# A ring of four output buffers and a newly searched issue order in a fused attention and feed-forward kernel

## The chip, the cores and the metric

The kernel runs on one core of a Trainium2 chip. Its time is device time in microseconds (us). Before the change it takes 350.42 us, the median of three runs (350.24 to 351.2). A core has a matrix engine, TensorE (PE in the profile, with its weight loads listed apart as PEld); a vector engine, VectorE (DVE); a scalar engine for activations, ScalarE (ACT); GpSimd (POOL) and SyncE (SP), which here do little but issue transfers. Each engine works through its own queue in order. PE writes into PSUM, a memory of eight banks of 128 x 512 float32; all other buffers are in SBUF, 128 partitions wide.

## The reference

Two stages. First an attention whose softmax is replaced by features: with `q`, `k`, `v` of 8 batches x 8 heads x 576 positions x 64 and `w_phi` of 64 x 128,

```python
def phi(x):
    proj = np.einsum('bhsd,df->bhsf', x, w_phi)
    proj = proj - np.max(np.abs(proj), axis=-1, keepdims=True)
    return np.concatenate([np.exp(proj), np.exp(-proj)], axis=-1)
q_p, k_p = (phi(q), phi(k))
kv = np.einsum('bhsf,bhsd->bhfd', k_p, v)
z = np.sum(k_p, axis=2)
num = np.einsum('bhsf,bhfd->bhsd', q_p, kv)
den = np.einsum('bhsf,bhf->bhs', q_p, z)[..., None] + 1e-06
attn = num / den
```

Then the heads are put side by side, giving 4608 tokens of 512, and a feed-forward layer follows: `h = max(x @ w_in, 0)`, `out = (h * h) @ w_out`, with `w_in` of 512 x 2048 and `w_out` of 2048 x 512. The output is 4608 x 512 in float32.

## The kernel before

The function builds a plan of 1738 operations and then issues them in a fixed order. Each `add` names an engine, a cost, the buffers read (`r`) and written (`w`), and the PSUM bank that the operation opens or closes. `plan.arrange` applies four tables that an offline search has left at the end of the file. `ORDER` is the order of issue of all operations, so it sets the queue of each engine. `BASES` gives the PSUM bank of each opened group. `STATES` chooses between ACT and DVE for 231 copies and relus that either can do (`either`). `GATES` names, for each load on POOL, the operation that it has to wait for. A fifth table, `FILL`, puts runs of dummy matmuls on zeros ahead of named operations: `85: (0, 26)` is 26 of them into bank 0 ahead of operation 85. Operations are named by their number in the plan in what follows.

An operation's buffers come from the framework, which adds the waits: an instruction that uses a PSUM bank or an SBUF buffer waits for what used it before in the order of issue, where one of the two writes, and two engines' accesses to one PSUM bank are put one behind the other even where both only read.

**Attention**, one batch of 576 positions x 8 heads at a time (18 blocks of 128 columns). `xk`, `xq`, `xv` are the loads (L245 and others, POOL). `kT` and `qT` hold the transposed inputs: for batches 0 and 1 PE transposes them (L316) and DVE or ACT copies them out; for batches 2 to 7 one DMA transpose each, issued on SP, does it. L342 is the projection of four blocks into two PSUM banks; its two row halves use 64 of the array's rows at a time. Of each projection DVE takes the maximum of the absolute value (L397 for keys into `mk`, L501 and L534 for queries into `mq`) and ACT the two exponentials (L403 into `kp` and `kn`; L547 into `qf`, or from a second projection with the operands exchanged, L572, the exponentials of L587 into `qpn`). The value rows are scaled by exp of the maxima (L416 and L422 on ACT, L430 on DVE, into `va`), L463 makes `kv`, which is copied out by L192 or L190. L651 multiplies query features with `kv`, the positive half first; DVE scales that half in PSUM (L663), the negative half is added, DVE takes the reciprocal of the denominators (L673) and writes the tokens `xo` (L677). A DMA transpose on SP (L711, operations `Xx`) brings `xo` into `xT`, for batch 0 PE and a copy do (the first tile of all in two halves, `out_halves`).

**Feed-forward**: chunk c is the first 512 tokens of batch c; the ninth chunk is the 8 x 64 positions left over, gathered in `xS`. Per chunk 16 groups of four matmuls (L797) make the hidden layer, ACT or DVE applies the relu into `hr` (L774, L776), DVE squares it into `h2` (L783). For chunk 0 the groups are cut smaller, so that they can begin with the first tokens (L822 in halves, L808, L836). Four groups of 16 matmuls (L891) make an output tile of 128 tokens; L192 or L190 copies it out of PSUM into a buffer of the ring `ot` of three, and SP stores it (L909, L906 for the ninth chunk). The very last tile of 36 is made in two unequal halves (L855), copied by ACT (L871) and DVE (L869) into a buffer of its own, `otl`, and stored in four pieces over SP and ACT (L878).

The chunks and the next batch's attention are woven into one another by `ORDER`. In SP's queue the stores of output tiles stand between the transposes; around 66 to 80 us the order there is query transpose 396, transposes of tokens 297 and 306, store 519, transpose of tokens 315, store 537.

## Time and the profile before

The profiled execution took 351.15 us; its span, from the first to the last instruction, is 349.2 us.

| | |
|---|---|
| median of three runs | 350.42 us (350.24 to 351.2) |
| profiled execution | 351.15 us, span 349.2 us |
| PE, matmuls | 336.7 us, 96% of the span |
| DVE | 272.0 us, 78% |
| ACT | 229.6 us, 66% |
| POOL | 96.2 us, 28% |
| moved to and from memory | 46.2 MB (36.77 MB read, 9.44 MB written), 132 GB/s over the span |

Busy shares are those of an engine's instructions over the whole span, and a busy PE also counts dummy matmuls and the modelled ends of pipelined ones. Idle time ahead of an instruction is put down to what ended it. In a view of groups each line has the busy time, the mean duration in nanoseconds, and the idle time ahead with its most frequent releaser. In the timeline a square bracket holds the idle time ahead of an instruction and what ended it; a `q` behind an engine's name is its queue of transfers. In the table by stages the columns are PE, weight loads, DVE, ACT and POOL (busy us and instructions in brackets), then granted PE clock, share of the DMA engines and GB/s.

### The profile page before, as it was taken

To read this page: it belongs to the slowest core of one execution; us is meant where nothing else is said; L and a number is where in the kernel's file an instruction comes from. 1 tells how busy PE (TensorE), PEld (TensorE's weight loads), DVE (VectorE), ACT (ScalarE), POOL (GpSimd) and SP (SyncE) were. 2 spreads that over 40 slices of the span, in tenths; PEclk is the share of its full clock that TensorE was granted. 3 is DMA by queue.
4 is the path that set the end of the run, shared out by engine and by line. 5 is a ranking of instruction groups with operands and counts; after the bars stand their busy time and mean duration, and the time that the engine had idled before them with its cause. 6 is when DMAs were issued, how large, how long until landed. Compare 5 with 4: busy or idle time off the path is not lost.

```text
span 349.2 us, 8405 instructions
## 1 busy us (share of the span) xinstructions
PE 336.7 (96%) x3323; PEld 192.3 (55%) x3353; DVE 272.0 (78%) x518; ACT 229.6 (66%) x434; POOL 96.2 (28%) x144
## 2 busy tenths in 40 slices
PE   6999999999999999999999999999999999999994
PEld 5878866544654555446555554465555554444443
DVE  2999999889988979898989995998889735653251
ACT  3999897789978995877698788584785403232011
POOL 8844352283361835060600130360000000000000
PEclk9999999999999999999999999999999999999998
DMA  8999999898997999899999999999785422000025
GB/s 90 178 201 200 203 120 147 137 194 129 146 163 159 148 155 147 173 163 210 165 196 189 227 154 150 206 142 161 157 153 145 90 47 98 32 0 30 0 92 121
DMA packets 133623, 49.05 MB, mean 140 GB/s; under 512 B 102096, under 2 KB 129104, under 8 KB 133584
## 3 DMA queue, kind: packets, MB, share of 16 engines
q0 software_dynamic: 45232, 18.36, 45.9%
q1 hardware_dynamic: 88112, 29.99, 42.6%
q8 instruction: 26, 0.43, 0.5%
q10 hardware_dynamic: 240, 0.16, 0.1%
q14 instruction: 13, 0.11, 0.1%
HBM read 36.77 MB, written 9.44 MB: 132 GB/s over the span
## 4 chain that ended last, share of the span: by engine, by line
PE 84%; DVE 7%; DMA 3%; ACT 3%; issue 2%; POOL 1%; POOLq 0%; DVEq 0%; ACTq 0%
PE psum L891 32%; PE psum L797 31%; PE psum L651 5%; PE psum L342 5%; PE psum L458 4%; DVE va L430 2%; PE psum L836 2%; DMA xk<-in_k_dram 1%; DMA xT<-xo 1%; PE psum L572 1%; PE psum L822 1%; PE psum L808 1%; DVE mq L501 1%; PE psum L855 1%; PE psum L463 1%
## 5 line engine op out<-in xcount | busy, mean ns | idle before, releaser
L891 PE MATMUL psum<-wout,h 128*128 128x512 bf16 x530 | 129.6, 379 | 2.3 <-issue 1.1
L797 PE MATMUL psum<-xT,win 128*128 128x512 bf16 x448 | 106.7, 379 | 0.3 <-DMA xT<-xo 0.2
L774 ACT ACTIVATE hr<-psum 128x512 bf16<-128x512 f32 x97 | 56.5, 598 | 53.9 <-PE psum L797 28.4
L891 PEld LDWEIGHTS <-h 128*128 128x128 bf16 x560 | 50.7, 97 | 54.9 <-issue 0.6
L797 PEld LDWEIGHTS <-win 128*128 128x128 bf16 x512 | 47.2, 97 | 52.5 <-issue 1.8
L783 DVE TENSOR_TENSOR h<-hr 128x512 bf16<-128x512 bf16 x144 | 56.7, 415 | 12.4 <-ACT hr L774 11.8
L776 DVE TENSOR_SCALAR hr<-psum 128x512 bf16<-128x512 f32 x47 | 32.0, 686 | 19.2 <-PE psum L797 17.7
L547 ACT ACTIVATE qf<-psum 128x1024 bf16<-128x1024 f32 (+1 forms) x40 | 36.2, 937 | 10.2 <-DVE mq L534 9.4
L403 ACT ACTIVATE kp<-psum 128x1024 bf16<-128x1024 f32 (+1 forms) x35 | 32.9, 941 | 12.8 <-DVE mk L397 12.5
L397 DVE TENSOR_REDUCE mk<-psum 128x8 f32<-128x1024 f32 (+1 forms) x35 | 38.7, 1110 | 2.5 <-PE psum L342 2.3
L587 ACT ACTIVATE qpn<-psum 128x1024 bf16<-128x1024 f32 (+1 forms) x40 | 36.5, 945 | 3.4 <-PE psum L572 3.4
L651 PEld LDWEIGHTS <-qpn 128*128 128x128 bf16 x624 | 27.6, 97 | 13.3 <-issue 0.8
L430 DVE TENSOR_TENSOR va<-xv,va 64x256 bf16<-64x256 bf16 (+2 forms) x66 | 30.1, 470 | 4.1 <-ACT va L422 3.5
L403 ACT ACTIVATE kn<-psum 128x1024 bf16<-128x1024 f32 (+1 forms) x35 | 32.7, 938 | 0.0
L663 DVE TENSOR_TENSOR psum<-psum,en 128x520 f32<-128x520 f32 (+1 forms) x39 | 27.3, 701 | 6.9 <-PE psum L651 5.2
L245 POOL DMA_DIRECT2D xv<-in_v_dram x27 | 19.8, 742 | 39.2 <-ACT va L416 11.6
L651 PE MATMUL psum<-kv,qpn 128*128 128x65 bf16 x624 | 30.2, 193 | 0.2
L245 POOL DMA_DIRECT2D xk<-in_k_dram x28 | 20.4, 742 | 35.4 <-PE psum L463 16.4
L677 DVE TENSOR_TENSOR xo<-psum,rden 128x512 bf16<-128x512 f32 (+1 forms) x39 | 26.7, 686 | 1.0 <-DVE rden L673 0.2
L534 DVE TENSOR_REDUCE mq<-psum 128x8 f32<-128x1024 f32 (+1 forms) x20 | 22.2, 1113 | 2.0 <-PE psum L342 1.1
L192 ACT ACTIVATE ot<-psum 128x512 f32<-128x512 f32 x20 | 12.0, 598 | 17.8 <-PE psum L891 15.8
L501 DVE TENSOR_REDUCE mq<-psum 128x8 f32<-128x1024 f32 (+1 forms) x20 | 22.0, 1110 | 1.8 <-PE psum L342 1.8
(79 smaller groups left out, 389.2 us busy)
## 6 DMA issues: line engine op xcount, KB each, us to landing
out_dram<-ot SPq DMA_DIRECT2D x32, 256.0 KB, 2.9
xk<-in_k_dram POOLq DMA_DIRECT2D x26, 128.0 KB, 4.7
xq<-in_q_dram POOLq DMA_DIRECT2D x24, 128.0 KB, 4.6
xv<-in_v_dram POOLq DMA_DIRECT2D x24, 128.0 KB, 4.6
win<-in_moe_w_in_dram POOLq DMA_DIRECT2D x4, 512.0 KB, 11.3
wout<-in_moe_w_out_dram POOLq DMA_DIRECT2D x4, 512.0 KB, 13.5
xq<-in_q_dram POOLq DMA_DIRECT2D x4, 256.0 KB, 8.2
out_dram<-ot SPq DMA_DIRECT2D x6, 128.0 KB, 2.4
```

What stands on the lines that cost most here:

```text
L245: pin(nc.gpsimd.dma_start(out=x[:, a * 512 : z * 512].rearrange("p (h x) -> p h x", x=4 * D), in_=src[b][2 * a : 2 * z, 0:512, :].rearrang ...
L397: pin(nc.vector.tensor_reduce(out=mk_view(g), in_=ps2(pj)[:, :, : n * Fd].rearrange("p e (i f) -> p e i f", f=Fd), axis=AX.X, op=ALU.max, ...
L403: pin(nc.scalar.activation(out=dst[slot][:, :, :n, :].rearrange("p e i f -> p e (i f)"), in_=ps2(pj)[:, :, : n * Fd], func=ACT.Exp, scale= ...
L430: pin(nc.vector.tensor_tensor(out=t[:, :, :D].rearrange("p m (x c) -> p m x c", c=2), in0=x.rearrange("p (m x c) -> p m x c", m=n, c=2), i ...
L547: pin(nc.scalar.activation(out=o, in_=i_, func=ACT.Exp, scale=sgn))
L587: pin(nc.scalar.activation(out=o, in_=i_, func=ACT.Exp, scale=sgn))
L651: pin(nc.tensor.matmul(out=o[:, u // 4, u % 4 * D1 : (u % 4 + 1) * D1], lhsT=qpn[slot][:, sg * half + u * m : sg * half + u * m + P], rhs= ...
L774: pin(nc.scalar.activation(out=hr[sl], in_=ps1(g), func=ACT.Relu))
L776: pin(nc.vector.tensor_scalar(out=hr[sl], in0=ps1(g), scalar1=0.0, scalar2=None, op0=ALU.max))
L783: pin(nc.vector.tensor_tensor(out=dst, in0=i_, in1=i_, op=ALU.mult))
L797: pin(nc.tensor.matmul(out=o, lhsT=win[mc // 4][:, kc, mc % 4 * P : (mc % 4 + 1) * P], rhs=x, start=(kc == 0), stop=(kc == KC - 1)))
L891: pin(nc.tensor.matmul(out=ps1(g), lhsT=h2[c % 2][mc // 4][:, mc % 4, tt * P : (tt + 1) * P], rhs=wout[mc // 4][:, mc % 4, :], start=(mc = ...
```

## The change

Three things in the code, and the tables anew.

The output ring has four buffers, and the last tile's `otl` is no buffer of its own any more: it is slot `SL` of the ring, (36 - 1) % 4 = 3. The half copies into it name that slot as written, and the store of the slot's user before names it as read, so that the framework and the plan keep them apart.

The maxima and the exponentials of one projection no longer name its PSUM bank as written but as locked (`lock`), a word that only the offline search reads: the order table may put a maximum ahead of or behind the exponentials of the same bank. Before, the plan fixed it: maximum, positive exponential, negative exponential.

`ORDER`, `BASES`, `STATES` and `GATES` are replaced as a whole, and `FILL` has eight runs with 107 dummies in place of eleven with 133.

```diff
-    def add(self, eng, cost, fn, r=(), w=(), opens=None, closes=None, dma=None, tiled=False, release=False, what=""):
+    def add(self, eng, cost, fn, r=(), w=(), opens=None, closes=None, dma=None, tiled=False, release=False, what="", lock=None):
         op = Op(eng, cost, fn, opens, closes, dma, tiled, release, len(self.ops), what)
+        op.lock = lock
...
-    ot = ring("ot", 3, [DM], F32)
-    otl = sb("otl", [DM], F32)
+    NOT = 4
+    ot = ring("ot", NOT, [DM], F32)
+    SL = (B * S // P - 1) % NOT
+    otl = ot[SL]
...
-            add("DVE", dve_cost(2 * n * Fd), fn, r=[pj], w=[pj] + [("mk", s2, g, e) for e in range(2)], what="Mk")
+            add("DVE", dve_cost(2 * n * Fd), fn, r=[pj], w=[("mk", s2, g, e) for e in range(2)], lock=pj, what="Mk")
...
-                add("ACT", act_cost(2 * n * Fd), fn, r=[pj], w=[pj] + [(nm, slot, e) for e in range(2)],
-                    closes=pj if sgn < 0 else None, what="E" + nm)
+                add("ACT", act_cost(2 * n * Fd), fn, r=[pj], w=[(nm, slot, e) for e in range(2)], lock=pj, what="E" + nm)
...
-            add("DVE", dve_cost(2 * n * Fd), fn, r=[pj], w=[pj, ("mq", s2, c)], what="Mq")
+            add("DVE", dve_cost(2 * n * Fd), fn, r=[pj], w=[("mq", s2, c)], lock=pj, what="Mq")
...
-                w=[("otl", half)], closes=gs[half], what="oth")
+                w=[("otl", half), ("ot", SL, half)], closes=gs[half], what="oth")
...
-            sl = oslot[0] % 3
+            sl = oslot[0] % NOT
...
-                add("SP", (0.5, 0), fn, r=[("ot", sl)], dma=(0.37 if c == NCH - 1 else 0.74, HW_IN, "st"), what="st")
+                add("SP", (0.5, 0), fn, r=[("ot", sl)] + [("ot", SL, half) for half in range(2) if sl == SL],
+                    dma=(0.37 if c == NCH - 1 else 0.74, HW_IN, "st"), what="st")
...
 FILL = {
-    85: (0, 26), 87: (1, 2), 41: (3, 8), 63: (7, 16), 106: (7, 9), 65: (7, 10), 116: (7, 37), 110: (7, 7),
-    144: (7, 3), 234: (7, 12), 122: (2, 3),
+    85: (0, 26), 108: (1, 29), 65: (7, 12), 43: (7, 7), 110: (7, 7), 147: (7, 8), 172: (7, 16), 135: (7, 2),
 }
```

Of the new tables, what the prediction speaks of: in SP's queue around the first stores, the order was 395, 288, 396, 297, 306, 519, 315, 537, 592, 324, 593, 555 and is 395, 288, 396, 306, 297, 315, 537, 592, 593, 555, 519, 324. Operation 7, a clear of a part of `va` on DVE, moves from place 143 of the order to the eleventh. Of the 231 choices between ACT and DVE, 96 change. The last stores on SP were 1709, 1708, 1722, 1723, 1716, 1715, 1734, 1736 and are 1715, 1722, 1716, 1708, 1709, 1723, 1734, 1736.

## The prediction

> **What bounds the kernel now.** I read the page's busy shares first, then busy time by stage, then the waits, then the chain of waits and the timeline where a wait stood out.
>
> Busy shares:
>
> ```profile
> PE 336.7 (96%) x3323; PEld 192.3 (55%) x3353; DVE 272.0 (78%) x518; ACT 229.6 (66%) x434; POOL 96.2 (28%) x144
> ```
>
> TensorE has 349.2 - 336.7 = 12.5 us without a matmul. Busy time by stage shows where they lie:
>
> ```profile
> 0.00:10.00 10.00, 6.74 (x72) 5.91 (x72) 3.75 (x12) 3.91 (x8) 8.91 (x17) 1.00 0.92 100
> 10.00:20.00 10.00, 9.97 (x160) 8.39 (x158) 9.37 (x18) 9.55 (x27) 8.21 (x12) 1.00 1.51 186
> 20.00:30.00 10.00, 9.05 (x171) 7.01 (x168) 9.98 (x26) 9.66 (x17) 3.80 (x6) 1.00 1.38 200
> ...
> 30.00:66.00 36.00, 35.15 (x524) 27.21 (x528) 33.60 (x68) 30.31 (x62) 14.21 (x21) 1.00 1.16 159
> 66.00:80.00 14.00, 13.29 (x117) 6.31 (x117) 12.01 (x20) 12.35 (x19) 8.22 (x12) 1.00 1.20 166
> 80.00:340.00 260.00, 257.89 (x2257) 134.66 (x2280) 202.20 (x378) 162.70 (x304) 52.88 (x78) 1.00 0.81 135
> ```
>
> The columns are PE, weight load, DVE, ACT, POOL. Until 30 us the busy PE means little, because dummy matmuls fill it; there DVE (9.37 and 9.98 of 10) and ACT (9.55 and 9.66) are full and set the pace. From 30 to 340 us PE is idle for 0.85 + 0.71 + 2.11 = 3.7 us, and that is the most that any order could return there. The rest is the head and the last 9 us.
>
> The densest loss is at 66 to 80. Waits, then the chain and the timeline there:
>
> ```profile
> ACT ot L192 <- DMA out_dram<-ot: 2.0, 2, 1.2
> PE psum L572 <- ACT qpn L587: 0.5, 1, 0.5
> PE psum L797 <- DMA xT<-xo: 0.2, 1, 0.2
> ```
>
> ```profile
> 68.47 4.74 DMA xT<-xo
> ...
> 73.89 1.65 ACT qpn L587 x2
> ```
>
> ```profile
> 67.77 0.58 SPq L909 DMA_DIRECT2D out_dram<-ot  x1
> 68.47 1.21 SPq L711 DMA_TRANSPOSE xT<-xo  x1
> ...
> 73.10 0.60 ACT L192 ACTIVATE ot<-psum 128x512 f32<-128x512 f32 x1 [1.23 <-DMA out_dram<-ot]
> 73.25 1.52 PE L797 MATMUL psum<-xT,win 128*128 128x512 bf16 x6 [0.18 <-DMA xT<-xo]
> ...
> 75.58 0.39 PE L572 MATMUL psum<-qT,wphi 64*128 64x512 bf16 x2 [0.48 <-ACT qpn L587]
> ```
>
> The fourth output copy (op 572) sat 1.23 us on ACT until the first tile's store had landed, because the ring has three buffers. Behind it in ACT's queue stood the exponentials of L587, and PE waited 0.48 us for those. The transpose into xT was issued behind that same store on SP's queue, and PE waited 0.18 us for it.
>
> **The change part by part.** The sum is made against the profiled execution: span 349.2, time 351.15, which is 0.73 above the median of the three runs (350.42). I apply it to the median.
>
> *Ring of four.* Op 572 takes slot 3, never used before, so its wait goes: 1.23 us earlier on ACT. L587's exponentials move up with it, and in the new ACT list two of the small exponentials (417 and 418, 0.21 each) have moved behind them. Of L572's 0.48 nothing should stay. On SP's queue the store 519 now stands far behind transpose 315 instead of ahead of it, so 315 goes out 0.70 earlier and the 0.18 goes too. What is late next: 457 then follows its PE predecessors, and transpose 306 still waits for the query transpose 396 (2.74 on SP). The stage's whole idle time is 0.71, which bounds the gain. I take -0.7, ends -0.9 (a little of the cost lies in late starts that aren't recorded as idle) and 0. The other wait of this kind (0.74 at 106.3) delays nothing that PE waited for: 0. The last tile's two half copies now take slot 3 instead of a buffer of their own, so they wait for the store of the tile that used slot 3 before them, four tiles earlier. That store goes out at about 337.4 in before's order and a store of this kind lands 2.9 later, at 340.3; the half copies come at 343.8 (L871) and 344.7 (L869): 3.5 us of room, so 0; if the room were gone, up to those 2.9.
>
> *Free order of maxima and exponentials.* Nothing is added or removed. The waits that it can touch are ACT's, on L397 (12.5 us in 13) and L534 (9.4 in 7). After 30 us they are hidden by PE, which is full: 0. Before 30 us they are part of the next item.
>
> *The head, order and dummies.* I compared the two lists engine by engine. Up to the copy that the first feed-forward products wait for (op 143, the copy of the second transposed half into xT, L632 to L635), exactly the same DVE instructions stand ahead; up to op 177 on ACT, exactly the same ACT instructions. DVE is full from 7.9 us on, so the head can only move by DVE's idle time. One clear of 0.28 (op 7) moves from DVE's full stretch to its idle start: -0.28. In before DVE's one large gap is 0.46, ahead of a maximum at 12.87, where PE had ten dummies (0.72) in the way. In after 12 dummies stand there, and op 58 waits for an exponential (about 0.4, from 0.27 starts of half-size exponentials on ACT), so that gap is replaced rather than removed. I take -0.2; ends -0.8 (all of DVE's small gaps between 10 and 20, 0.63, and the clear) and +1.0 (two new gaps like the old one).
> The dummies fall from 133 to 107 matmuls. The run of 37 that goes (2.24 us at 13.43) lay beside a DVE that never stopped, so its end gains nothing: 0. If the cover goes, meaning that PE becomes the head's bound, it would be worth up to 2.
>
> *PE's own work.* The matmuls are the same. Each step between 64-row and 128-row matmuls leaves about 0.10 between the weight loads (12.44 + 0.22 to 12.76, against none between equal ones). There are 106 such steps before and 104 after: -0.2, ends the same.
>
> *Engines chosen anew.* 96 of 231 choices change. Relu: 36 to DVE, 29 to ACT. kv copies: 11 to DVE, 3 to ACT. Output copies: 10 to ACT, 3 to DVE. Net on DVE 7 x 0.69 + 8 x 0.42 - 7 x 0.68 = +3.4 us, against 77 idle over the span. By stage it is narrower. Up to op 323 (about 71 us) DVE carries 2 more relus, 2 more kv copies and 2 fewer output copies, some +0.6; up to op 414 (about 77 us) two more relus and two squares of 0.42 come on top, about +3 in all. DVE's idle time in 30 to 80 is 2.4 + 2.0 = 4.4. I take 0, ends -0.7 and +2.0.
>
> *Loads.* Each POOL load is gated anew. Many gates move forward by 5 to 40 us. The tightest (op 386) opens some 5 us of PE work before the transpose 396 that needs it; such a piece takes 0.7 to issue and 4.6 to land, so it is just covered: 0, ends 0 and +0.4.
>
> *Tail.* In before the stores of the first finished of the last whole tiles went out last, and SP issued six stores in 3.73 us, to 344.7, just ahead of the final two (345.12). In after they go first, SP is free about 0.6 earlier, but ACT's last store (1.34 from 344.29) then ends the span: -0.2, ends -0.3 and 0.
>
> Sum: -0.7 - 0.2 - 0.2 + 0 - 0.2 = -1.3, so 350.42 - 1.3 = 349.1.
>
> **The clock and a rule.** The first 26 dummies load at 2.69 / 25 = 0.108 us apart, the 37 at 13.42 at 2.07 / 36 = 0.057, so the array runs at half rate until about 9 us. The Trainium skill (TensorE: Matmul & The Clock Gate, "HAM oscillation — how this bites in real kernels") says that the gate falls back to half rate after PE gaps of more than about 3.4 us. By that rule fewer dummies cost nothing, since I find no stretch of over 1.2 us between PE's remaining work in the new list's head, and the sum stays at 349.1; the trace of before has a 2.2 us gap ahead of 5.9 us but was at half rate anyway, so no run here shows the fall.
>
> **The rivals.**
> *Ring's gain given back.* L797 would then wait for xT all the same: the transpose took 4.74 to land here against a median of 3.0, so what lands it may be the DMA engines (DMA share 1.20 in that stage), not the issue. For it: the stage's transfers don't change. Against: 0.70 earlier issue. Then -0.1 instead of -0.7: 349.8, no change by measurement.
> *Slower: DVE becomes the bound at 30 to 80.* The place is the maxima L397 and L501 and the scaled products L663, which PE waits on. 3 us more work meets 4.4 us of idle; it decides once over 1.4 us of that idle lies where PE's late results put it. Against: the new list puts squares and maxima between each L663 and the reciprocal after it, where the old one idled (0.28, 0.23, 0.65). If 2 us fall on PE: 350.42 - 0.6 + 2.0 = 351.8.
> *Clock falls in the head with fewer dummies.* Some 24 query projections on DVE's path at 0.051 more each: +1.2, 350.3.
> *Better than forecast:* the head gives its -0.8: 348.5.
>
> **How the numbers follow.** A difference of 0.3% (1.05 us) is about what a measurement of this kernel can tell from none. Forecast at 349.1: 0.42; its own spread puts a fifth of that above 349.37. Head better, 348.5 or lower: 0.15. Gain given back: 0.15. Clock: 0.05. DVE bound: 0.23. Faster: 0.34 + 0.15 = 0.49, same: 0.08 + 0.15 + 0.05 = 0.28, slower: 0.23. The range: below, -0.9 - 0.8 - 0.2 - 0.3 = -2.2 with -0.7 from new engines gives 347.5; above, the DVE case with the ring's gain lost too, 350.42 - 0.2 + 2.0 = 352.2.
>
> **What would show it.** ACT's output copy near 73 us without a wait on its store, and PE's idle time in 66 to 80 under 0.3: ring right. First feed-forward product (L822, at 29.11 in before) between 28.4 and 29.3: head right. DVE busy over 95% with PE waiting on L397, L501 or L663 in 30 to 80: the slower rival. Dummies at 0.107 apart after 10 us: the clock. It is wrong above all if PE idles for new waits after 80 us, where I have checked the lists only for loads and gates and for the work ahead of PE, not each bank.

## The result, and the profile after

The changed kernel takes 362.82 us (median of four runs, 360.84 to 366.91) against 350.42: slower, by a ratio of 1.033 (95% interval 1.028 to 1.038), which leaves out the slowest of the four, a slow run. The forecast was 349.1, within 347.5 to 352.2. The profiled execution took 366.91 us, that slowest run, with a span of 365.1 us; a second profile of the same kernel (364.47 us, run e0 below) has the same two stalls.

Busy shares of the changed kernel, the line that was shown of before:

```profile
PE 342.3 (94%) x3327; PEld 192.9 (53%) x3327; DVE 273.8 (75%) x526; ACT 229.3 (63%) x426; POOL 96.3 (26%) x144
```

TensorE has now 365.1 - 342.3 = 22.8 us without a matmul, where it had 12.5. Busy time by stage of the changed kernel, columns as before:

```profile
30.00:66.00 36.00, 33.44 (x500) 26.00 (x497) 32.81 (x68) 27.90 (x53) 14.17 (x21) 1.00 1.23 159
66.00:80.00 14.00, 10.79 (x86) 5.11 (x88) 6.50 (x11) 6.83 (x12) 2.13 (x4) 0.76 0.69 110
80.00:340.00 260.00, 252.29 (x2268) 131.26 (x2263) 201.79 (x377) 167.21 (x306) 57.62 (x85) 0.99 0.90 135
```

The column behind POOL is the granted clock: 0.76 between 66 and 80 us, where it was 1.00. The waits of PE, with the total, the number and the longest, have two new entries at the top:

```profile
PE psum L797 <- ACT hr L774: 6.7, 1, 6.7
PE psum L345 <- DMA kT<-xk: 5.8, 1, 5.8
```

Each is one wait. The timeline around them shows what was late (L345 is L342 of the kernel before, L329 is L326):

```profile
58.30 5.12 SPq L329 DMA_TRANSPOSE kT<-xk  x1
...
69.21 0.61 PE L345 MATMUL psum<-wphi,kT 64*128 64x128 bf16 x8 [5.77 <-DMA kT<-xk]
```

```profile
157.93 14.70 SPq L551 DMA_TRANSPOSE qpn<-qf  x2
...
162.33 1.02 ACT L547 ACTIVATE qf<-psum 128x1024 bf16<-128x1024 f32 x1 [6.42 <-DMA qpn<-qf]
167.14 1.02 ACT L547 ACTIVATE qf<-psum 128x1024 bf16<-128x1024 f32 x1 [3.58 <-DMA qpn<-qf]
168.06 0.59 ACT L774 ACTIVATE hr<-psum 128x512 bf16<-128x512 f32 x1
168.71 1.87 PE L797 MATMUL psum<-xT,win 128*128 128x512 bf16 x4 [6.74 <-ACT hr L774]
```

First stall: the transpose of batch 2's keys (operation 395) was issued at 58.30 and PE could start its products at 69.21. Second stall: PE needed a bank that a relu on ACT had to read; that relu stood behind exponentials (L547) whose buffer was still being read by feature transposes (851 and 839). In the list of transfers between 48 and 72 us, with the median time from issue to landing in the last place, the keys' transpose of the changed kernel reads

```profile
kT<-xk SPq DMA_TRANSPOSE x1, 10.9
```

and in the kernel before

```profile
kT<-xk SPq DMA_TRANSPOSE x1, 5.1
```

Nothing of the transpose itself had changed. Seven loads were in flight with it at some time, two on the average. The two slowest of these took 10.0 (386) and 5.5 us (392) to land, where the loads of keys of this size land in 4.6 in the median. The query transpose 396, which reads what 386 brings, was next on SP from 64.7 us on and went out at 69.08, when 386 had landed.

In the second stall 851 did not only land late (7.9 us). Its data were ready at 150.3 us and it was issued at 154.3, behind the transpose of batch 5's keys (986), which waited for its last load, 969, until 151.4.

To see all of it I followed how late PE is: the start of each of its operations less the sum of PE's own work ahead of it (the pitch of its weight loads, by kind). The difference between two points is what was lost there.

| PE's work done, us | lost before | lost after | difference |
|---|---|---|---|
| up to 44 | 18.56 | 18.17 | -0.39 |
| 44 to 48 (first stall) | 0.20 | 8.48 | +8.28 |
| 48 to 60 (the output copy's wait) | 1.20 | 0.17 | -1.03 |
| 60 to 130 | 1.66 | 2.41 | +0.75 |
| 130 to 140 (second stall) | 0.41 | 9.59 | +9.18 |
| 140 to the last operation of PE | 4.06 | 3.63 | -0.43 |
| from there to the end | 5.10 | 4.68 | -0.42 |
| sum | | | +15.94 |

The spans differ by 365.1 - 349.2 = 15.9. Two places carry 17.5 of it, and everything else together is 1.5 us faster, where the forecast had 1.3.

### The profile page after: what moved, and what is told of

Its sections match the earlier page's. It is cut to its first block, busy times and chain, and to the rows that moved or that the text cites. A ratio compares the mean times of both kernels' runs of the same rounds, so it can differ in the third digit from the quotient of the medians.

```text
span 365.1 us, 8340 instructions
## 1 busy us (share of the span) xinstructions
PE 342.3 (94%) x3327; PEld 192.9 (53%) x3327; DVE 273.8 (75%) x526; ACT 229.3 (63%) x426; POOL 96.3 (26%) x144
## 3 DMA queue, kind: packets, MB, share of 16 engines
q0 software_dynamic: 45232, 18.36, 44.7%
HBM read 36.77 MB, written 9.44 MB: 127 GB/s over the span
## 4 chain that ended last, share of the span: by engine, by line
PE 81%; DMA 9%; ACT 6%; DVE 2%; issue 1%; SPq 0%; DVEq 0%; ACTq 0%; POOLq 0%
PE psum L891 30%; PE psum L797 30%; PE psum L651 5%; PE psum L345 5%; PE psum L458 4%; DMA qpn<-qf 3%; DMA kT<-xk 3%; PE psum L836 2%; DMA xT<-xo 1%; ACT qpn L587 1%; ACT kn L387 1%; DMA xk<-in_k_dram 1%; ACT kp L387 1%; PE psum L572 1%; PE psum L808 1%; PE psum L855 1%
## 5 line engine op out<-in xcount | busy, mean ns | idle before, releaser
L891 PE MATMUL psum<-wout,h 128*128 128x512 bf16 x560 | 135.5, 383 | 0.0
L774 ACT ACTIVATE hr<-psum 128x512 bf16<-128x512 f32 x90 | 52.4, 598 | 48.9 <-PE psum L797 37.7
L797 PEld LDWEIGHTS <-win 128*128 128x128 bf16 x512 | 48.1, 99 | 61.3 <-issue 10.4
L783 DVE TENSOR_TENSOR h<-hr 128x512 bf16<-128x512 bf16 x144 | 55.6, 415 | 13.7 <-ACT hr L774 13.3
L547 ACT ACTIVATE qf<-psum 128x1024 bf16<-128x1024 f32 (+1 forms) x40 | 36.3, 937 | 18.0 <-DMA qpn<-qf 10.0
L398 DVE TENSOR_REDUCE mk<-psum 128x8 f32<-128x1024 f32 (+1 forms) x35 | 38.5, 1106 | 12.1 <-PE psum L345 8.8
L776 DVE TENSOR_SCALAR hr<-psum 128x512 bf16<-128x512 f32 x54 | 36.5, 684 | 12.7 <-PE psum L797 7.8
L663 DVE TENSOR_TENSOR psum<-psum,en 128x520 f32<-128x520 f32 (+1 forms) x39 | 27.3, 701 | 9.3 <-PE psum L651 7.0
L195 ACT ACTIVATE ot<-psum 128x512 f32<-128x512 f32 x27 | 16.1, 595 | 27.1 <-PE psum L891 26.9
L534 DVE TENSOR_REDUCE mq<-psum 128x8 f32<-128x1024 f32 (+1 forms) x20 | 22.1, 1109 | 6.5 <-ACT qf L547 4.8
L268 POOL DMA_DIRECT2D xq<-in_q_dram x24 | 17.3, 722 | 36.7 <-DMA qT<-xq 8.9
```

What stands on the lines that cost most here:

```text
L398: pin(nc.vector.tensor_reduce(out=mk_view(g), in_=ps2(pj)[:, :, : n * Fd].rearrange("p e (i f) -> p e i f", f=Fd), axis=AX.X, op=ALU.max, ...
L547: pin(nc.scalar.activation(out=o, in_=i_, func=ACT.Exp, scale=sgn))
L774: pin(nc.scalar.activation(out=hr[sl], in_=ps1(g), func=ACT.Relu))
L776: pin(nc.vector.tensor_scalar(out=hr[sl], in0=ps1(g), scalar1=0.0, scalar2=None, op0=ALU.max))
L783: pin(nc.vector.tensor_tensor(out=dst, in0=i_, in1=i_, op=ALU.mult))
L797: pin(nc.tensor.matmul(out=o, lhsT=win[mc // 4][:, kc, mc % 4 * P : (mc % 4 + 1) * P], rhs=x, start=(kc == 0), stop=(kc == KC - 1)))
```

## The experiments

The question was what made the transposes late. Theory: they share the DMA engines with loads, and the new gates and the new order of loads put loads beside them (collision). Rivals: they are issued too late, or in a queue behind something else, whatever the loads do. The kernel before was run beside each, so ratios are compared, not times of different chips. A loss "between 44 and 48 us of work" is a line of the table above, worked out in the same way for the profile of each run.

| run | median, us | ratio to before (95%) |
|---|---|---|
| the changed kernel again (e0) | 362.69 | 1.029 (1.023 to 1.035) |
| e1, first stall's loads moved | 358.14 | 1.013 (1.009 to 1.017) |
| e2, second stall's loads moved | 354.85 | 1.008 (1.003 to 1.012) |
| e3, both | 353.47 | 1.002 (0.998 to 1.007) |
| e4, dummies in the first stall | 356.63 | 1.011 (1.007 to 1.015) |
| e6, kernel before with four loads put beside transpose 395 | 355.84 | 1.013 (1.009 to 1.017) |
| e8, e1 and early keys | 352.83 | 1.004 (1.001 to 1.007) |
| e11b, e1 and another order on SP | 352.44 | 1.003 (0.9995 to 1.006) |
| e11, the same, seven gates missing | 352.22 | 1.004 (1.001 to 1.007) |
| e12b, e3 and that order on SP | 350.07 | 0.997 (0.994 to 0.9997) |
| e12, the same, seven gates missing | 349.46 | 0.996 (0.994 to 0.999) |
| e9, e3 and early keys | 349.43 | 0.995 (0.993 to 0.997) |
| e10b, e9 and three loads later | 350.85 | 0.999 (0.996 to 1.002) |
| e10, the same, seven gates missing | 350.85 | 0.999 (0.996 to 1.002) |
| e5, kernel before with the ring of four | 351.60 | 1.002 (0.999 to 1.004) |
| e5b, the same with one store moved | 353.85 | 1.006 (1.004 to 1.009) |

A slip of mine has to be told first. When I wrote the tables of e10, e11 and e12, the gates of seven loads (578, 589, 779, 969, 980, 1368, 1377) got lost, so that these three kernels differ by more than the edit meant, and what was expected of them was written without knowing it. 969 is the load that a transpose in question waits for. e10b, e11b and e12b are the edits alone, run later; the readings below rest on them, and the three first ones stand beside them.

**The changed kernel itself**, with no edit.

> The changed kernel itself, on the chip of the runs that follow. Both theories: two stalls of PE, near 63 and near 162 us, each followed by a stretch at half clock where the gap is over 3.4 us; 358 to 367 us, and more spread from run to run than the kernel before, since the latency of the transposes sets the time.

359.29 to 366.42, median 362.69. PE waited 3.7 us at the first place and 7.0 at the second, with 395 at 8.7 us to landing, 851 and 839 at 7.4 and 9.8. The stalls come back in this profile too, with another size.

**First stall, loads moved (e1).** Loads in POOL's order, and the operation that a load waits for:

```diff
 ORDER
-    377, ..., 384, ..., 578, ..., 394, ..., 385, ..., 587, ..., 392, ..., 386, ..., 401
+    377, 384, 385, 386, 578, ..., 401, 394, 587, 392
 GATES
-    385: 281, 386: 361, 578: 263, 394: 220, 587: 49, 392: 115
+    385: 219, 386: 219, 578: 219, 394: 401, 587: 401, 392: 401
```

> The changed kernel with loads moved around its first stall (PE without work from 63.2 to 69.0 us): the loads 394, 587 and 392 wait for the first product that reads the transposed keys (401), and 384, 385, 386 and 578 go out right behind 377. The keys' transpose 395 keeps its place and, since the loads that it waits for keep theirs, its issue at about 58. Theory, collision: 395 took 10.9 us to land in place of 5.1 because four loads were still in flight with it; with only the tail of three left it lands in 5 to 6.5, at 63 to 64.5, PE waits under 1.4 us, its clock does not fall, and the kernel gains 6 to 8.5 us (about 355 against 362.8). Rival, lateness: 395 is 2.25 us later than in the kernel before and slow by itself at that place; then the wait stays at 5 to 6 us and the time changes by less than 1 us.

```profile
57.12 3.42 SPq L329 DMA_TRANSPOSE kT<-xk  x1
...
62.84 0.23 PEld L345 LDWEIGHTS <-kT 64*128 64x128 bf16 x8
```

In its timeline 395 goes out at 57.12 and lands in 5.3 us, and PE starts its products without a wait. Between 44 and 48 us of work PE lost 0.20, as in the kernel before, in place of 8.48. The issue also moved, by 1.2 us, so that alone could not have done it: 10.9 us from 57.1 would have ended at 68. The second stall stayed (6.2 us of wait, 9.4 lost). The rival, that 395 is slow by itself there, falls. The time fell by 4.7 us, less than the 6 to 8.5 expected.

**The same collision in the kernel before (e6).** Four loads of values, from 70 to 74 us before, are put behind load 576:

```diff
 ORDER
-    576, ..., 391, ..., 389, ..., 390, ..., 392
+    576, 389, 390, 391, 392
 GATES
-    389: 402, 390: 298, 391: 375, 392: 320
+    389: 254, 390: 254, 391: 254, 392: 254
```

> The kernel before, with four loads of values (389 to 392) moved from 70 to 74 us to right behind load 576, near 54.6 to 57.4, so that they are in flight together with the keys' transpose 395 (issued at 55.8, landed in 5.1). Theory, collision: 395 lands 3 to 6 us later, at 64 to 67, PE waits 0.5 to 3.5 us for it at 401 (63.5), the kernel becomes 0.5 to 4 us slower. Rival, the order of the changed kernel is needed for it: 395 lands within 1 us of 60.9 and the time is the same or, for the loads that are taken out of 70 to 74, a little less.

The timeline of this kernel, and its line in the list of transfers from 48 to 72 us:

```profile
55.61 4.61 SPq L326 DMA_TRANSPOSE kT<-xk  x1
...
67.22 0.42 PE L342 MATMUL psum<-wphi,kT 64*128 64x128 bf16 x8 [3.67 <-DMA kT<-xk]
```

```profile
kT<-xk SPq DMA_TRANSPOSE x1, 11.6
```

395 goes out 0.45 us earlier than in the kernel before (56.06) and lands in 11.6 us, not 5.1; the two loads that overlap it most (391, 392) take 8.9 and 10.1. PE loses 5.5 us between 44 and 48 us of work, and the kernel is 1.3% slower, more than I had expected (0.5 to 4 us). So loads put beside the transpose are enough to make the stall, without anything else of the change.

**The price by itself (m1).** A kernel of nothing but transfers, which computes nothing of the reference. Each phase has so many loads and stores beside the transpose; stores and transpose wait for a first load:

```diff
+PHASES = [(0, 0), (1, 0), (2, 0), (4, 0), (6, 0), (0, 2), (0, 4)] * 3
...
+        l0 = load(lead, 0)
...
+        for i in range(loads):
+            now.append(load(xv[i], i + 1).ins.name)
+        for i in range(stores):
+            c, t = divmod(n % 3 * 12 + i * 3, 4)
+            s = pin(nc.scalar.dma_start(out=out[c * 512 : c * 512 + 512, :].rearrange("(p j) n -> j p n", j=4)[t], in_=ot))
+            dep(s, l0.ins.name)
...
+        x = pin(nc.sync.dma_start_transpose(out=kT, in_=xs))
+        dep(x, l0.ins.name)
```

> The disputed cost by itself; all of the computation is left out and the output is zeros. Per phase one leading load of 128 KB, then, issued when it has landed, one transpose of 128 x 2304 values, with 0, 1, 2, 4 or 6 further loads issued right behind the leading one, or with 2 or 4 stores of 256 KB issued with it; each phase three times, one phase after the other. Theory, collision: about 4.5 to 5 us alone, 0.5 to 1.5 us more per load in flight, 8 to 12 us with 6, and the loads that meet the transpose are stretched too. Rival: the transpose takes the same within 1 us up to 6 loads, and what delayed it in the kernel was something else (PE's and ACT's traffic, or the fetching of instructions). If the stores delay it as much per KB as the loads, it is the traffic; if not, it is the loads' own kind.

Time of the transpose from issue to landing in the second and third pass, and how many loads were in flight with it on the average:

| beside it | nothing | 1 load | 2 | 4 | 6 | 2 stores | 4 stores |
|---|---|---|---|---|---|---|---|
| us | 4.5, 4.5 | 4.5, 4.5 | 5.2, 4.9 | 6.6, 6.6 | 10.9, 9.7 | 6.1, 6.0 | 9.1, 9.0 |
| loads in flight | 0 | 0.2, 0.2 | 0.7, 0.7 | 1.8, 1.9 | 3.1, 3.1 | 0 | 0 |

In the first pass the kernel's final stores ran between the phases and the loads were issued long before the transpose, and had mostly landed, or did so soon after, when it began. There it took 4.6 us with one, two and four loads and 5.8 with six, 1.9 of them in flight on the average; with the stores it took 6.8 and 8.6.

With six loads in the second and third pass the last two, issued behind the transpose, take 8.4 to 9.9 us. The sizes seen in the kernels (10.9 and 11.6) are reached here too. But the number of loads doesn't settle the price: transpose 395 took 10.9 us in the changed kernel with 2.0 loads in flight on the average, transpose 790 in the kernel before 7.7 with 4.1. Two stretches of this kernel, the transpose alone and the transpose with six loads, have in the last three columns granted clock, the DMA engines' busy share and GB/s:

```profile
84.00:88.50 4.50, 0.00 (x0) 0.00 (x0) 1.00 0.70 131
...
119.40:130.00 10.60, 0.00 (x0) 1.95 (x3) 1.00 1.18 124
```

Together the engines are busier and move no more by this count. But the count takes a load by the bytes that it writes, 128 KB of bf16, and it reads 256 KB of float32 for them: on the page of the changed kernel the loads' queue has 18.36 MB where 36.77 MB were read from memory. Four stores, 1 MB, cost the transpose 4.5 us, with 194 GB/s moved. Six loads cost 5.2 to 6.3 us for 0.79 MB written or 1.57 MB read: more per KB than the stores by the one count, no more by the other. So these runs don't tell whether it is the traffic or something in the loads' own kind.

**Second stall, loads moved (e2), and both (e3).** For e2 the five loads that were issued beside 851 and 839 go behind relu 919; e3 has the edits of e1 and e2.

```diff
 ORDER
-    1174, ..., 1167, ..., 975, ..., 985, ..., 974, ..., 977, ..., 919
+    919, 977, 975, 974, 985, 1174, 1167
 GATES
-    1174: 810, 1167: 850, 975: 746, 985: 748, 974: 460
+    1174: 919, 1167: 919, 975: 919, 985: 919, 974: 919
```

> The changed kernel with loads moved around its second stall (PE without work from 161.9 to 168.7 us): the five loads 1174, 1167, 975, 985 and 974, issued from 154.5 to 157.2, go behind 977 and wait for relu 919. Theory, collision: the feature transposes 851 and 839 (7.9 and 9.1 us to landing, 6.4 us of issue for the second) were slowed by these loads and ACT, which needs their source buffers again, stood 6.4 + 3.6 us; without the loads they land in 4.5 to 6 us, PE waits under 1.5 us and the kernel gains 7 to 9.5 us (about 354.5 against 362.8). Rival, order of ACT: two buffers for three sets of exponentials are too few where the new order puts the third set 2 us behind the second, whatever the loads do; then PE still waits over 4 us and the gain is under 3 us.

> Both edits together. Theory, collision: the gains add, 13 to 18 us, and the kernel comes out at 346.5 to 350, at or below the 350.4 of the kernel before, since outside the two stalls the changed kernel's PE work is ahead of the old one's (0.3 us after the head, 1.3 us between 66 and 80). Rival, DMA volume: a stall only moves to the next transpose that waits behind the postponed loads, and more than half of the gain is lost again (over 355).

In e2 851 and 839 landed in 4.5 us each, and the loss between 130 and 140 us of work fell from 9.6 to 1.9, but 4.05 were lost right behind: the next feature transpose, 863, now met the postponed loads and took 10.3 us. The time was what had been expected (354.85 for about 354.5), in part by chance: in this profile the first stall, which e2 leaves alone, cost a wait of 3.2 us and no fall of the clock, so the time doesn't price the second stall by itself. In e3, 851 and 839 took 4.3 and 4.6 us, and PE still waited:

```profile
PE psum L797 <- ACT hr L774: 3.4, 1, 3.4
```

PE lost 5.6 us between 130 and 140 us of work, and the kernel came out at 353.47 where 346.5 to 350 were expected: clean transposes were not enough. In e3's trace 851's data were ready at 141.3 us and it was issued at 147.0:

```profile
143.62 3.27 SPq L329 DMA_TRANSPOSE kT<-xk  x1
147.00 1.74 SPq L551 DMA_TRANSPOSE qpn<-qf  x1
```

It stood on SP behind the transpose of batch 5's keys, 986, which waited for load 969 (landed at 143.5). That load was one of five behind load 1171 on POOL, which waited for transpose 790 (9.6 us to landing, with loads beside it) because it overwrites what 790 reads.

**The queue.** e8 puts the two loads early (with the first stall's loads moved, the five loads of e2 left where they were); e11b leaves all these loads and changes only the order on SP; e9 and e12b do the same on top of e3.

```diff
 ORDER, e8 and e9
-    1166, ..., 1169, ..., 1165, ..., 1171, ..., 973, ..., 969, ..., 787
+    969, 973, ..., 1171, ..., 787, 1166, 1169, 1165
 GATES, e8 and e9
-    969: 812
+    969: 650
 ORDER on SP, e11b and e12b
-    986, 851, 913, 839
+    851, 913, 839, 986
 GATES, e11 and e12 besides (the slip)
-    578: 219, 589: 535, 779: 717, 969: 812, 980: 333, 1368: 1312, 1377: 1131
```

> The changed kernel with the first stall's loads moved as before, and for the second stall only this: the last two loads of batch 5's keys, 969 and 973, go out ahead of 1166 (near 121 us in that run's time) and the loads 1166, 1169 and 1165 of the batch after take their place behind 787. The five loads 1174 to 974 stay where they were. Theory, queue: 851 stood 5.7 us behind the keys' transpose 986 in SP's queue, which waited for load 969, which stood on POOL behind a load that waited for transpose 790; with the loads early 986 issues near 137, 851 and 839 right after their exponentials, ACT's two waits (4.5 and 2.1 us with both earlier edits) end and PE's wait behind them is under 1.5 us with no fall of the clock: 349 to 351. Rival, collision alone: the five loads still meet 851 and 839, these land as late as before and PE still waits over 3.4 us with a fall of the clock: 353.5 to 358.

> All three moves of loads together. Theory: neither stall is left, the work of PE is about 1.5 us ahead of the kernel before up to 60 us and 1 to 1.5 at the end: 348.5 to 350. Rival: the five postponed loads delay query transpose 987 and the values of batch 5, and over 2 us are lost behind 160 us: 351 or more.

> The changed kernel with the first stall's loads moved, and for the second stall no load moved: only the keys' transpose 986 goes behind the feature transpose 839 on SP. Theory, queue: 851 and 839 stood ready while 986 waited for load 969; now they go out right behind their exponentials, at about 142 and 144 us, before the five loads 1174 to 974, and PE's wait near 152 falls from 6.2 us to under 2 without a fall of the clock: 349.5 to 352.5. Rival, collision alone: 851 or 839 still take 7 us or more beside loads, PE's wait stays over 3.4 us and the clock falls: 354 to 358.

> The first stall's loads moved, the five loads of the second moved, and 986 behind 839 on SP; the keys' loads 969 and 973 stay where they were. Theory: both causes of the second stall are away and the time is that of the three moves of loads, 349 to 350.5. Rival: the late keys' transpose 986 delays the products of batch 5's keys (988, near 159 us) and over 1.5 us are lost there: 351 to 353.

> e11 as I had described it: e1 with the batch-5 keys' transpose 986 behind 839 on SP, and nothing else. The run e11 had lost the gates of seven loads besides (578, 589, 779, 969, 980, 1368, 1377), 969 among them, the load that 986 waits for. If the order on SP alone mends the queue: 851 is issued near 142 us or earlier, PE's wait behind the relu is under 1 us, the loss between 130 and 140 us of PE's work is 2.5 to 4.5 us (e11: 3.6), ratio 1.001 to 1.007. If the lost gate of 969 did part of it: 986 now comes later than in e11, PE's wait for the keys is over 4 us, and the ratio is 1.007 to 1.013, near e1's 1.013.

> e12 as I had described it: e3 with 986 behind 839 on SP, all gates kept. If loads moved and order on SP are enough: ratio 0.993 to 0.999, under 1 us lost between 130 and 140 us of PE's work, as in e12. If e12 owed its gain to the seven lost gates: ratio 0.999 to 1.004, as e3 (1.002), with PE waiting over 2 us for the relu or for batch 5's keys.

In e8, 986 goes out at 138.4 and 851 follows at 142.5, 4.8 us to landing; 839 still meets the five loads and takes 7.5. PE waits, in its list of waits,

```profile
PE psum L797 <- ACT hr L774: 2.0, 1, 2.0
```

with no fall of the clock, and the loss between 130 and 140 us of work is 2.8. The kernel at 352.83 lies between what the theory (349 to 351) and the rival (353.5 to 358) expected. In e11b, with only the order on SP changed, 851 goes out at 141.9 and lands in 4.7 us, 839 takes 7.9, and PE's wait for the relu is 1.0; but 986, now behind them, overlaps seven loads in flight and takes 13.9 us, and PE waits for that:

```profile
PE psum L345 <- DMA kT<-xk: 2.7, 1, 2.7
```

Its loss there is 4.6, just over the 2.5 to 4.5 that I had expected. The missing gates of e11 changed little: there 969 went out at 135.7, in e11b at 134.9, so its gate had been passed either way, and e11 lost 3.6.

So the queue was the larger part of the second stall and the loads the rest: of the 9.4 us of e1, 2.8 (early keys) or 4.6 (order on SP) are left with the queue mended; with the loads mended and the queue not, 5.6 (e3); with both, 0.5 (e9 and e12b). The two parts add up to about the whole, but they aren't independent: a later 986 meets the loads. Both kernels with all of it are ahead of the kernel before, e9 by 0.5% (0.3 to 0.7), e12b by 0.3%, with an interval that ends just short of nothing (0.03 to 0.6). In e9's waits the line of the second stall reads

```profile
PE psum L797 <- ACT hr L774: 0.5, 1, 0.5
```

and its span is 347.2 us against 349.2 in the profile of before.

**Later still (e10b).**

```diff
 ORDER
-    1174, 1167, ..., 1180, ..., 1366
+    1366, 1174, 1167, 1180
 GATES, e10 besides (the slip)
-    578: 219, 589: 535, 779: 717, 969: 650, 980: 333, 1368: 1312, 1377: 1131
```

> All three moves of loads, and in addition the loads 1174, 1167 and 1180 behind 1366, so that the feature transpose 863 (8.9 us with six loads in flight in the run before this) and the query transpose 987 meet three loads fewer. Theory, collision: 863 lands 2 to 4 us earlier, the wait of ACT behind it (2.5 us) goes, and 0.3 to 1 us is gained over the run with three moves (348.4 to 349.2 against 349.4). Rival: PE does not depend on 863 there, or the postponed loads of keys delay transpose 1183: the same within 0.3 us, or slower.

> e10 as I had described it: e9 with the loads 1174, 1167 and 1180 behind 1366, all gates kept. If these loads hold transpose 863 and that costs PE time: 863 lands in under 7.5 us (e9: 8.9) and the ratio is 0.990 to 0.994. If 863 has slack there: ratio 0.994 to 0.997, as e9. If the 0.4% by which e10 was behind e9 came from the edit and not from the lost gates: 0.997 to 1.002 again.

863 took 7.7 us where e9's took 8.9, but nothing was gained: 0.999 (0.996 to 1.002), as with the gates missing. Between 140 and 150 us of work PE lost 0.6 where e9 lost 1.2; between 150 and 170 it lost 2.4 (1.2 in e10) where e9 lost 0.5, most of it in one wait for exponentials of keys; on ACT these stand behind an exponential that waited 2.1 us for a feature transpose:

```profile
183.26 0.40 PE L651 MATMUL psum<-kv,qpn 128*128 128x65 bf16 x8 [1.68 <-ACT kp L404]
```

The postponed loads go out at 166 to 167 instead of 155 to 156, and load 1173 behind them then takes 8.5 us where it took 6.7. That the new wait comes from them fits, but no run here takes them apart.

**Dummies in the first stall (e4).**

```diff
 FILL
+    401: (4, 90),
```

> The changed kernel with 90 dummy matmuls (about 5 us) put into the first stall, ahead of product 401, into the bank that 401 opens. The wait for the keys' transpose stays. Theory, clock: after that wait the granted clock is 0.78 for 10 us and PE loses another 2.4 us; with the array at work through most of the wait the clock stays at 1.00 around 70 to 80 us and the kernel gains 1.5 to 3 us (about 360.4 against 362.8). Rival: the slow stretch behind the wait is not the wait's doing, the clock falls all the same and the time stays within 0.7 us, or is longer by what the dummies add.

Stretches of five microseconds of the changed kernel, and of e4; the granted clock is the third number from the right:

```profile
65.00:70.00 5.00, 0.79 (x11) 0.49 (x12) 0.14 (x1) 0.00 (x0) 0.00 (x0) 0.75 0.93 85
70.00:75.00 5.00, 5.00 (x22) 1.96 (x20) 2.65 (x5) 3.02 (x5) 0.00 (x0) 0.56 0.87 167
```

```profile
65.00:70.00 5.00, 4.84 (x86) 4.49 (x84) 0.55 (x1) 0.39 (x1) 0.00 (x0) 1.00 0.73 81
70.00:75.00 5.00, 5.00 (x48) 2.50 (x46) 4.15 (x8) 4.43 (x8) 0.00 (x0) 1.00 0.93 124
```

With the array at work the clock stays, and PE does 48 matmuls from 70 to 75 us where it did 22. The whole kernel gained more than this place can give: in its profile the second stall, which e4 leaves alone, cost a wait of 1.2 us only, and five of its runs (355.4 to 356.8) lie near the profiled one, three at 361 to 362. So its time doesn't price the clock. The rows do: 0.25 x 5 + 0.44 x 5 = 3.5 us of array time. Of the 8.28 us of the first stall 5.77 are the wait, and about 2.5 were lost behind it.

**The ring of four alone (e5, e5b).** The code of the change with all tables of the kernel before. In e5 the store 573 stands behind the copy 769 into the same buffer, so one output tile is stored with the later tile's values; e5b moves that store ahead.

```diff
 ORDER, e5b
-    769, ..., 573
+    573, 769
```

> The kernel before with the code of the change and all its own old tables: only the ring of four and the shared last slot. Forecast's reason: the output copy 572 no longer waits 1.23 us and PE's 0.48 at product 457 goes, 0.18 behind transpose 315 stays (the order on SP is the old one): 0.3 to 0.6 us faster. Rival: what was queued behind waits for something else and nothing is gained (within 0.2 us). Neither theory of the stalls expects one here: PE's longest wait between 30 and 340 us stays under 1 us.

> The kernel before with the ring of four alone, its own tables, and one store (573) moved ahead of the copy that reuses its buffer (769). Theory: PE gains 1.0 to 1.4 us between 66 and 106 us, as in the earlier run of this edit, and gives it back near 205 to 210 us where PE waits for exponentials that wait for feature transpose 1072: within 0.5 us of the kernel before. Rival: the loss at 210 us was chance and the kernel is 0.8 to 1.4 us faster.

In e5 PE loses 0.14 us between 48 and 60 us of work where the kernel before loses 1.20: the ring does give 1.06. At the end it is all gone (1.002, 0.999 to 1.004). It went at one place, where ACT waits for a feature transpose that is no earlier:

```profile
208.85 2.86 ACT L547 ACTIVATE qf<-psum 128x1024 bf16<-128x1024 f32 x3 [1.33 <-DMA qpn<-qf]
210.84 0.62 PE L345 MATMUL psum<-wphi,kT 64*128 64x128 bf16 x16 [1.26 <-ACT qf L547]
```

In e5b the moved store brought a wait of its own, since the copy 769 now needs it landed, and the kernel became 0.6% slower; the timeline of e5b:

```profile
106.72 0.60 ACT L195 ACTIVATE ot<-psum 128x512 f32<-128x512 f32 x1 [2.85 <-DMA out_dram<-ot]
...
107.37 1.43 PE L891 MATMUL psum<-wout,h 128*128 128x512 bf16 x4 [2.12 <-ACT ot L195]
```

## Why the prediction was wrong

**The step that failed is "Loads".** It had 0, ends 0 and +0.4, and the two stalls cost 17.5 us. It took the time of a load (4.6 us to land) and that of a transpose as fixed, and asked only whether the tightest load, 386, would still be there for its reader 396. The runs show three things in its place. Loads in flight make a transpose beside them late: 395, which 386 meets, took 10.9 us, and 5.3 with the loads moved away (e1). They become late themselves: 386 took 10.0 us, so it was not covered, and 396 went out 4.3 us after SP was free for it (PE was waiting for 395 all that time, so that cost nothing more). And a late load holds what stands behind its reader: 986 waited for load 969 until 151.4 us, and 851, ready at 150.3, stood behind 986 in SP's queue until 154.3. A row for the first stood in the trace of before: transpose 790 took 7.7 us with four loads in flight on the average, 986 took 4.6 with none.

**What made the collision costly was the slack.** In before, 395 landed 2.7 us ahead of its first product; in e5, with the same tables, it took 7.0 us and still cost PE nothing. In the changed kernel 395 was issued 2.2 us later (58.30 for 56.06, its last load having landed at 58.1), and the same product was wanted 0.1 us after a normal landing.

**For the second stall the step "Engines" has a part that no run isolates.** Relu 919, for which PE waits there, was on DVE before and is on ACT now, behind the third set of exponentials of a batch, with two buffers for their results. I looked at the balance between DVE and ACT, and not at what each queue would wait for there. No run changes this order alone; e9 keeps it and loses 0.5 us there, so without late transposes it costs little. The text named the risk (new waits after 80 us), but gave it no chance of its own and no price.

**Ring of four**: -0.7 forecast, -1.03 measured in its stage, -1.06 when done alone. The mechanism was right, the size beyond the -0.9 that was its end: recorded idle time did not bound the gain. That the gain could be given back stood among the rivals, but at another place: alone it is lost at 210 us, not at 73.

**The head**: -0.2 forecast. The first feed-forward product is at 28.57 us, within the stated 28.4 to 29.3. Over all profiles it starts at 28.0 to 29.7 with the new head (14 profiles, mean 28.7) and 28.5 to 29.1 with the old (4 profiles, mean 28.8), so a gain of 0.2 is neither shown nor excluded.

**Tail**: -0.2 forecast, -0.42 measured. **Mode switches** (-0.2) weren't measured by themselves. **Slower because of DVE**: no. In the changed kernel none of PE's long waits is on L398 (the old L397), L501 or L663, but the first stall hides what DVE's load would do. In e9, without the stalls, DVE is busy 47.1 of 50 us between 30 and 80 (45.6 before), just short of the 95% named as a sign, and PE has no wait on it there.

**The clock.** My rival was a fall in the head for want of dummies. There was none in the changed kernel's profile; but in five of the 14 profiles with the new head the clock rose at 3.6 to 4.3 us, fell back at 7.1 to 7.7 and was full again from 10.5 to 11.1. Their first feed-forward products came at 28.8 to 29.2, where the three in which it rose at 4.3 to 4.6 and stayed had them at 28.0 to 28.3. In the changed kernel it fell behind the two stalls instead, 6.8 us at half rate each time. The rule that I cited (the Trainium skill, TensorE: Matmul & The Clock Gate, "HAM oscillation — how this bites in real kernels") did bear on this change, at gaps that I hadn't forecast.

Without the two stalls the sum comes out near: -1.3 forecast, -1.5 measured outside them. In part that is luck, since it holds +0.75 between 60 and 130 and -0.43 behind 140 that no term had. e9, which has the same code and order but for loads, is 0.5% faster than before.

## What to carry to other kernels

Where an order is searched with fixed transfer times, look at the slack that it leaves in front of each transfer that gates the bottleneck, and list what else is in flight beside it: a load that is on time for its own reader can still be what makes another transfer late. An engine's queue, SP's and POOL's too, is in order: find for each instruction that waits what stands ready behind it. Judge a step of such a change by its stage and by the end together, since a gain at one place is easily given back at the next transfer that didn't move.

## What the runs showed of the hardware

**Loads and transposes side by side.** In m1 a transpose of 128 x 2304 values takes 4.5 us alone, 6.6 with four loads (1.8 in flight on the average) and 9.7 to 10.9 with six (3.1 in flight). The loads issued behind it take 8.4 to 9.9 us, where the first load of a phase takes 3.0 to 3.3 in most of them. The Trainium skill (DMA: Bandwidth & Descriptors, "Rules for kernel authors") says that a transpose next to ordinary DMAs needs nothing; that is said of its result, and its time is another matter in these runs. While transpose 395 ran in the changed kernel, for some three microseconds from 62 us on the loads' queue moved 6 to 11 packets of mostly 512 bytes per half microsecond, 59 ns each: about what one engine can do. The same page ("Latency and other measured facts") tells of two engines that are usually slower, with a cause that it calls a guess; no run here shows which engines moved these packets.

**The clock is judged in windows, not by gaps.** In each profile the granted clock changes only at times that lie whole multiples of 3.41 us apart (in the changed kernel at 67.5 and 166.5, 29 times 3.41). I cut PE's time into these windows. In the middle of a run it fell after every window in which PE was busy for 38% or less, and after one with 45%; it didn't after windows with 46, 47, 52% and more. No sharp bound follows: in the first 8 us of five profiles it fell after windows with 40 to 49%, and near the end of two it didn't after windows with 44 and 45%. So a gap of 3.2 us in e2 that lay across two windows cost no clock, and one of 2.1 us in e5b that lay within one did. Every gap of 3.4 us or more in the middle of these runs did bring a fall, as the rule cited above says (the Trainium skill, TensorE: Matmul & The Clock Gate), but a shorter one can bring it too; the same page's "Part 1: The HAM clock gate" has the window of 3.41 us, free-running, and the trace agrees. The clock came back after the first window in which PE was busy for 90% or more (36 to 72% were not enough): 3.4 us when the wait ended in the window that brought the fall, 6.8 or 10.2 when it went on.

**Spread.** With the stalls in it the kernel runs from 359 to 367 us; without them (e9) from 348.3 to 351.6.
